# Keys and queries by one level of Strassen's recursion in a fused attention and feed-forward kernel

## The chip, the cores and the metric

The kernel runs on one core of a Trainium2 chip. The metric is the device time of one execution in microseconds (us). Engines are named as in the profile: PE is TensorE (matmuls), PEld its weight loads, DVE VectorE, ACT ScalarE, POOL GpSimd; SP issues most DMAs.

## The reference

x is 2048 x 512, with 32 heads of 16 columns and a hidden layer of 1792.

```python
x = A_x
xn = _layernorm(x, axis=-1)
s = _A_ref(xn, A_wqkv, A_wo)                  # softmax attention, 32 heads, then @ wo
g = _silu(_B_ref(xn, B_w1, B_b1, B_w2, B_b2)) # relu(xn @ w1 + b1)**2 @ w2 + b2
return x + s * g
```

Inside `_A_ref`, `qkv = x @ wqkv` (512 x 1536) gives the queries, keys and values that this change is about.

## The kernel before

All products in float32 accuracy are made from two parts: a value is split into a rounded high part and a low part (value minus high part), and a product is high x high + high x low + low x high. So one 128 x 512 output block with a contraction of 512 costs 3 x 4 = 12 matmuls of 128 x 128 on 512 columns, which accumulate in one PSUM bank (`linear`, line 112).

The front stage (lines 464 to 560) works through four chunks c of 512 tokens. For each it normalises x (`norm`, DVE, with the square root on ScalarE), transposes it on TensorE (`transpose`), and splits the result into high and low part (ScalarE casts, DVE subtracts). Then come four value tiles (`start_value`, `end_value`; stored through `vblocks`) and eight key and query blocks (`keyquery`, four groups g of 128 columns for each): 12 matmuls, a ScalarE cast to the high part, a DVE subtraction to the low part, a DMA to DRAM (`kdram`, `qdram`). PSUM has three tiles S of two banks and one bank each called lin and acc. The order of instructions is written out by hand (`manual_schedule`): every engine runs its own list in program order and waits only for data and for tiles to come free.

Between the key and query blocks lie the steps of the next chunk: `parts` is a generator over the normalisation, advanced by `next(parts)`; `split_w` makes the parts of the weights (ScalarE, GpSimd). The last chunk starts the first scores, the loads of K, Q and V (`load_ka`, `load_qa`, `load_v`), and the first pieces of the feed-forward weights (`load_piece`, `split_piece`).

The main loop follows: 64 turns of scores, exponentials (ScalarE), products with V (line 572) and, in between, the feed-forward and output matmuls (line 347), with the copies of some scores out of PSUM on DVE (line 322).

Of the kernel before, what the change touches and what calls it, by code (L numbers as in the profile page):

```python
# [48 lines left out]
def mha_ffn_kernel(ctx: ExitStack, tc: tile.TileContext, x, wqkv, wo, bx, w1, b1, w2, b2, out):  # L49
# [14 lines left out]
    xdram = [dram.tile([128, 2, 4, 512], FT, name=f"xd{c}") for c in range(3)]  # L64

# [4 lines left out]
    with tc.tile_pool(name="sb", bufs=1) as sb, tc.tile_pool(name="ps", bufs=1, space=PSUM) as ps:  # L70
        fast_path(tc, sb, ps, locals())
# [3 lines left out]
def fast_path(tc, sb, ps, env):  # L75
    nc = tc.nc
    ident, nvalid, stat = (env[n] for n in ("ident", "nvalid", "stat"))
    kdram, qdram, vdram, xdram, udram, zdram, gdram = (
        env[n] for n in ("kdram", "qdram", "vdram", "xdram", "udram", "zdram", "gdram"))
# [4 lines left out]
    BUFS = dict(S=3, KA=3, QA=2, P=8, T=2, ou=2, V=2, wr=2, u=2, st=2, mv=2, rs=2, zc=2, rc=2)  # L84
    cnt, turn, places = [0], {}, [0, 1, 2]

    def t(shape, dt, tag):

        cnt[0] += 1
        p = ps if tag in ("S", "lin", "acc") else sb  # L90
        if tag in BUFS:
            turn[tag] = turn.get(tag, -1) + 1
            n = turn[tag] % BUFS[tag]
            tag = f"{tag}{places[n] if tag == 'S' else n}"
        return p.tile(shape, dt, tag=tag, name=f"{tag}_{cnt[0]}")
# [30 lines left out]
    xload, xnorm, wraw, wsp, xT = {}, {}, {}, {}, {}  # L126

    def load_x(c):
        for i in range(2):
            a = xload[c, i] = t([128, 2, 512], FT, f"P{4 + 2 * (c % 2) + i}")  # L130
# [25 lines left out]
    def split_w(which, ks=range(4), parts="hl"):  # L156
        if which not in wsp:
            tiles = [[t([128, 2, 512], FR, f"P{8 + n}" if which == "v" and i else f"{w_tags[which]}{p}{i}")
                      for i in range(2)] for n, p in enumerate("hl")]
            wsp[which] = [[a[k // 2][:, k % 2] for k in range(4)] for a in tiles]  # L160
        for k in ks:
            raw, (h, l) = wraw[which][k // 2][:, k % 2], (p[k] for p in wsp[which])
            if "h" in parts:
                act.copy(h, raw)
            if "l" in parts:
                pool.tensor_tensor(l, raw, h.bitcast(FT), op=OP.subtract)

    def norm(c, tiles):
# [13 lines left out]
        s = t([128, 3, n], FT, "rs")  # L182
        sd, r, e = (s[:, j] for j in range(3))
# [6 lines left out]
        dve.scalar_tensor_tensor(r, e, 1.5, r, op0=OP.add, op1=OP.mult)  # L190
        for j in range(n):
            m = tiles[j]
            if m % 2 == 0:
                xnorm[c, m // 2] = t([128, 2, 512], FT, "T")
# [4 lines left out]
    def xT_tiles(c):  # L199

        if c % 2:
            xT[c] = [t([128, 4, 512], FR, f"x{p}") for p in "hl"]
        else:
            xT[c] = [t([128, 4, 512], FR, f"KA{j}") for j in range(2)]

    def transpose(c, i):
# [3 lines left out]
        pt = t([128, 4, 256], FT, "S")  # L210
        for j in range(2):
            for k in range(4):
                nc.tensor.transpose(pt[:, k, 128 * j:128 * j + 128],  # L213
                                    xnorm[c, i][:, j, 128 * k:128 * k + 128], ident)
        s = slice(256 * i, 256 * i + 256)
        if c:
            act.copy(h[:, :, s], pt)
        else:
            for j in range(2):
                act.copy(h[:, 2 * j:2 * j + 2, s], pt[:, 2 * j:2 * j + 2])  # L220
        for j in range(2):
            k = slice(2 * j, 2 * j + 2)
            dve.tensor_tensor(low[:, k, s], pt[:, k], h[:, k, s].bitcast(FT), op=OP.subtract)

    def transpose_tile(i):

        h, low = xT[0]
        pt = t([128, 4, 128], FT, "S")
# [3 lines left out]
        act.copy(h[:, :, s], pt)  # L232
        dve.tensor_tensor(low[:, :, s], pt, h[:, :, s].bitcast(FT), op=OP.subtract)

    def xpart(c, p, k):
        return xT[c][p][:, k]

    def save_xT(c):
        for p in range(2):
            sp.dma_start(xdram[c][:, p], xT[c][p].bitcast(FT))  # L240

    def start_value(c, i, tag="S", **kw):
        pv = t([128, 512], FT, tag)
# [7 lines left out]
    def end_value(c, i, v):  # L251
# [3 lines left out]
        vb = vblocks[n % 6]  # L255
        cast(act if i % 2 else dve, vb[:, :H * 17].rearrange("p (h e) -> p h e", e=17)[:, :, :DH],
# [3 lines left out]
    def keyquery(c, g, which, tag="S"):  # L260
        pk = t([128, 512], FT, tag)
        run(linear(pk, lambda p, k: wsp[which][p][k][:, 128 * g:128 * g + 128],
                   lambda p, k: xpart(c, p, k)))
        n = 2 * g + (which == "q")
        ev = t([128, 2, 512], FR, ("P2", "P3", "P4", "P5", "P6", "P7", "T", "T")[n] if c == 3 else f"P{n % 4}")
        split(ev[:, 0], ev[:, 1], pk, act, dve)
        dst = kdram[g][c // 2][:, :, 512 * (c % 2):512 * (c % 2) + 512] if which == "k" else qdram[g][c]
        sp.dma_start(dst, ev.bitcast(FT))

# [147 lines left out]
    def first(m):  # L417
# [10 lines left out]
        return [Block(lambda p, k, f=f: w[p][:, k, 128 * f:128 * f + 128], lambda p, k: x[p][:, k],  # L428
# [18 lines left out]
    def load_x_parts(c):  # L447
        xs[0] = [t([128, 4, 512], FR, f"x{p}") for p in "hl"]
        for p in range(2):
            sp.dma_start(xs[0][p].bitcast(FT), xdram[c][:, p])  # L450
# [16 lines left out]
    vblocks = [t([128, VW], FT, f"P{10 + i}") for i in range(6)]  # L467
# [4 lines left out]
    idle = t([128, 512], FT, "lin")  # L472
# [27 lines left out]
    firsts = [start_value(0, i, tag, todo=todo + late) for i, tag in enumerate(("lin", "acc"))]  # L500
    for i, n in ((0, 4), (1, 2), (0, 2), (1, 4), (0, 2), (1, 2), (0, 2), (1, 2)):
        more(firsts[i], n)
    transpose(0, 1)
    for i in range(2):
# [3 lines left out]
    for j in range(2):  # L508
        end_value(0, j, firsts[j])
    end_value(0, 2, third)  # L510
# [7 lines left out]
    parts = chain(norm(1, (0, 1)), norm(1, (2, 3)))  # L518
    for c in range(NC):
        for i in range(4):  # L520
            if c or i > 2:
                end_value(c, i, start_value(c, i))
                if c or i == 3:
                    next(parts, None)
# [546 lines left out]
```

## Time and profile before

| | |
|---|---|
| three runs | 1225.31, 1225.50, 1226.39 us; median 1225.5 |
| profiled execution, its own time | 1225.83 us |
| its span | 1224.1 us |
| granted TensorE clock | 0.998 |
| PE, DVE, ACT, POOL busy | 1213.3, 815.8, 1011.6, 278.8 us |
| last matmul of the front stage ends | 148.1 us |

The profile shows one execution, taken on the same core; the time beside the span is that of the whole launch on the device. A row of the groups has the line, engine, operation, output and input tiles, shapes and count, then busy us and mean ns of one, then the idle time before it and what ended it. A row of the timeline has start, duration, engine and line. Matmul durations overlap each other, since matmuls are pipelined; the pace is read from the chain.

### The profile page before, as it was taken

The page shows a single profiled execution, that of the slowest core. Times are in us where ns is not written, and L with a number is a line of the kernel's source. Part 1 is how long each engine was busy: PE and PEld are TensorE (multiplying, and loading weights), DVE is VectorE, ACT ScalarE, POOL GpSimd, SP SyncE. Part 2 cuts the span into 40 slices and gives each one's busy share as a digit, 9 for nine tenths or more (in the row PEclk, how much of TensorE's full clock was granted, in tenths as well). Part 3 has the DMA queues.
Part 4 walks back from the last instruction along what each step waited for, and adds up shares of the span by engine and source line. Part 5 has one row for each costly group of instructions (what it writes and reads, how often), then busy time and mean ns, then how long its engine had stood idle before and what let it go on. Part 6 is the DMA issues. An engine that isn't in the chain of part 4 may idle for free.

```text
span 1224.1 us, 24044 instructions
## 1 busy us (share of the span) xinstructions
PE 1213.3 (99%) x9925; PEld 716.3 (59%) x9925; DVE 815.8 (67%) x1302; ACT 1011.6 (83%) x1172; POOL 278.8 (23%) x222
## 2 busy tenths in 40 slices
PE   9999999999999999999999999999999999999997
PEld 8888755555555555555555555555555555555553
DVE  4542277676767775757686666676775758777776
ACT  4222489988889898888998888899898899899983
POOL 5000032122221230404022222131230403321222
PEclk9999999999999999999999999999999999999999
DMA  8675723232161223223423224151422233455434
GB/s 311 253 269 187 269 78 106 74 96 62 47 202 47 91 78 101 79 78 106 157 63 112 62 49 131 31 172 47 135 79 79 75 100 79 130 191 164 157 129 111
DMA packets 103543, 146.52 MB, mean 120 GB/s; under 512 B 42938, under 2 KB 57288, under 8 KB 101892
## 3 DMA queue, kind: packets, MB, share of 16 engines
q1 hardware_dynamic: 100772, 136.54, 35.5%
q0 software_dynamic: 2368, 7.87, 2.2%
q8 instruction: 79, 1.29, 0.4%
q10 hardware_dynamic: 288, 0.52, 0.1%
q14 instruction: 36, 0.29, 0.1%
HBM read 99.42 MB, written 45.47 MB: 118 GB/s over the span
## 4 chain that ended last, share of the span: by engine, by line
PE 99%; DVE 0%; ACT 0%; issue 0%; POOL 0%; POOLq 0%
PE acc L572 37%; PE spare L347 29%; PE S L299 15%; PE S L112 10%; PE acc L299 5%; PE lin L299 2%; PE lin L476 1%; PE S L213 1%; PE acc L112 0%; PE lin L112 0%; PE S L716 0%; DVE P L957 0%; DVE P L952 0%; PE spare L716 0%; PE S L230 0%
## 5 line engine op out<-in xcount | busy, mean ns | idle before, releaser
L303 ACT ACTIVATE P<-S 128x1024 f32<-128x1024 f32 x702 | 662.6, 1035 | 90.1 <-PE S L299 89.9
L572 PE MATMUL acc<-P,V 128*32 128x512 f32 x4096 | 453.5, 594 | 0.0
L322 DVE COPY P<-acc 128x512 f32<-128x512 f32 x322 | 222.7, 692 | 141.8 <-PE lin L299 71.3
L303 ACT ACTIVATE P<-P 128x1024 f32<-128x1024 f32 x322 | 314.5, 1082 | 0.0
L572 PEld LDWEIGHTS acc<-P,V 128*32 128x32 f32 x4096 | 126.1, 110 | 287.1 <-issue 265.5
L299 PE MATMUL S<-QA,KA 64*128 64x512 f32 x1404 | 289.7, 403 | 0.0
L322 DVE COPY P<-lin 128x512 f32<-128x512 f32 x322 | 220.5, 685 | 1.9 <-PE lin L299 0.6
L299 PEld LDWEIGHTS S<-QA,KA 64*128 64x128 f32 x1404 | 133.6, 184 | 109.8 <-issue 41.8
L105 POOL TENSOR_TENSOR wf1l<-wr,wf1h 128x1024 fp32r<-128x1024 f32 x28 | 68.4, 2443 | 289.1 <-ACT wf1h L99 112.1
L299 PE MATMUL acc<-QA,KA 64*128 64x512 f32 x322 | 127.3, 395 | 0.0
L299 PE MATMUL lin<-QA,KA 64*128 64x512 f32 x322 | 127.1, 395 | 0.0
L373 POOL MEMSET note<- 1x1 f32 x68 | 6.0, 88 | 397.7 <-PE spare L347 390.7
L347 PE MATMUL spare<-xl,wf1h 64*128 64x512 f32 x464 | 96.2, 391 | 0.0
L105 POOL TENSOR_TENSOR hl<-T,hh 128x1024 fp32r<-128x1024 f32 x28 | 80.0, 2859 | 52.9 <-DVE hh L101 51.1
L347 PE MATMUL spare<-xh,wf1l 64*128 64x512 f32 x480 | 91.6, 391 | 0.0
L347 PE MATMUL spare<-wf2l,hh 64*128 64x512 f32 x448 | 90.4, 390 | 0.0
L105 POOL TENSOR_TENSOR wf2l<-wr,wf2h 128x1024 fp32r<-128x1024 f32 x28 | 67.2, 2399 | 90.2 <-DVE wf2h L101 90.2
L598 DVE TENSOR_TENSOR ou<-acc,ou 128x512 f32<-128x512 f32 x31 | 21.4, 692 | 97.2 <-PE acc L572 85.4
L347 PE MATMUL spare<-wf2h,hl 64*128 64x512 f32 x448 | 83.5, 391 | 0.0
L347 PE MATMUL spare<-xh,wf1h 64*128 64x512 f32 x480 | 77.8, 392 | 0.0
L347 PE MATMUL spare<-wf2h,hh 64*128 64x512 f32 x448 | 72.0, 394 | 0.0
L299 PEld LDWEIGHTS acc<-QA,KA 64*128 64x128 f32 x322 | 59.3, 184 | 16.8 <-DVE P L322 2.3
(239 smaller groups left out, 1300.3 us busy)
## 6 DMA issues: line engine op xcount, KB each, us to landing
wr<-in_B_w_dram SPq DMA_DIRECT2D x56, 512.0 KB
KA<-kd SPq DMA_DIRECT2D x64, 256.0 KB
QA<-qd SPq DMA_DIRECT2D x128, 128.0 KB
kd<-P SPq DMA_DIRECT2D x15, 512.0 KB
qd<-P SPq DMA_DIRECT2D x15, 512.0 KB
u<-ud SPq DMA_DIRECT2D x15, 512.0 KB
V<-vd SPq DMA_DIRECT2D x8, 664.0 KB
vd<-P SPq DMA_DIRECT2D x16, 280.0 KB
```

The costliest lines, as they stand in the source:

```text
L105: leng.tensor_tensor(lo, src, hi.bitcast(FT), op=OP.subtract)
L112: mm(dst, lhs(a, k), rhs(b, k), start=n == 0, stop=n == len(todo) - 1)
L213: nc.tensor.transpose(pt[:, k, 128 * j:128 * j + 128], xnorm[c, i][:, j, 128 * k:128 * k + 128], ident)
L299: mm(dst, k[r, p, 128 * (kb % 8):128 * (kb % 8) + 128], q[r, p], start=True, stop=True)
L303: act.activation(ptile[i, p], src, AF.Exp, scale=SCALE)
L322: dve.tensor_copy(ptile[i, p][:, hp], sides[hp])
L347: ins = mm(bank, self.lhs(a, k)[r], self.rhs(b, k)[r], start=n == 0 and self.at[other] == 0, stop=n == len(self.todo[half]) - 1 and self.a ...
L373: f = pool.memset(note[:, notes[0]:notes[0] + 1], 0.0)
L476: mm(idle[:, :128], ident, ident, start=True, stop=True)
L572: mm(sides[0][32 * j:32 * j + 32], vq[qd][:, kb, 17 * j:17 * j + 32], ptile[i, j // 2][:, j % 2], start=first, stop=last)
L598: dve.tensor_tensor(ou, sides[0], part[0], op=OP.add)
```

## The change

- Keys and queries are made for two chunks at a time and for 256 columns at a time, as 2 x 2 blocks with a contraction of 2 x 256. Seven block products replace eight (the Winograd form of Strassen's recursion). A block product is 6 matmuls (`product`).
- For this, sums of the halves of x (T forms, `sums_x`, DVE) and of the weights (S forms, `sums_w`, DVE) are made and split into parts (ScalarE high, GpSimd low). The parts of the query S forms go to DRAM and come back for the second pair of chunks. The x forms live in `tforms`, the weight forms in `sforms`.
- The first product of the first chunk is made ahead (`first_products`, kept in SBUF by ScalarE), then `second_products` gives the first output block; `last_products` makes the other five products after the second chunk's values, adds them on DVE, and splits the results (ScalarE or, in the last group, DVE for the high part; GpSimd for the low part, which was DVE's).
- PSUM in the front stage is four banks B and four banks D; before the main loop they are closed and opened again as S0 and S1, then acc, lin and S2.
- ScalarE normalises chunks 1 to 3 and copies their values out of PSUM. The second half of the query weights is split on DVE. x is kept in four tiles rather than two, so that its DMAs are in halves. `vblocks` has three tiles rather than six.

The core of the diff:

```diff
+    BUFS = dict(S=2, D=4, B=4, KA=3, QA=2, P=8, ...)
...
-    def split_w(which, ks=range(4), parts="hl"):
+    def split_w(which, ks=range(4), parts="hl", engs=(act, pool)):
...
+        if c:
+            dve.scalar_tensor_tensor(b, mv[:, :, 0], -1.0, r, op0=OP.mult, op1=OP.mult)
...
+            if c:
+                act.activation(xnorm[c, m // 2][:, m % 2], xin[j], AF.Identity, bias=b[:, j:j + 1],
+                               scale=r[:, j:j + 1])
+                continue
...
     def transpose(c, i):
-        pt = t([128, 4, 256], FT, "S")
+        halves = [t([128, 2, 256], FT, "D") for _ in range(2)]
...
         for j in range(2):
+            act.copy(h[j][:, :, s], halves[j])
+        if c % 2:
+            plain[c, i] = halves, [t([128, 2, 2, 256], FT, f"P{2 + 2 * i + j}") for j in range(2)]
+            act.copy(plain[c, i][1][1][:, 0], halves[0])
+        for j in range(2):
+            dve.tensor_tensor(low[j][:, :, s], halves[j], h[j][:, :, s].bitcast(FT), op=OP.subtract)
...
-    def keyquery(c, g, which, tag="S"):
...
+    def product(dst, left, right):
+        todo = [(a, b, k) for a, b in ((0, 0), (0, 1), (1, 0)) for k in range(2)]
+        for n, (a, b, k) in enumerate(todo):
+            mm(dst, left[a][:, k], right[b][:, k], start=n == 0, stop=n == 5)
+
+    def sums_x(c, i, between=lambda: None):
...
+        sub(t1, f[0], h[0])
+        sub(t1, t1, l[0])
+        sub(t2, f[1], t1)
+        sub(t3, f[1], t3)
+        between()
+        def parts_of(ms):
+            for m, v in ms:
+                act.copy(tforms[m][0][:, :, s], v)
+            for m, v in ms:
+                sub(tforms[m][1][:, :, s], v, tforms[m][0][:, :, s].bitcast(FT), pool)
+        def fourth():
+            sub(t4, h[1], t2)
+            dve.tensor_tensor(t4, t4, l[1], op=OP.add)
+            parts_of([(3, t4)])
+        parts_of([(1, t2), (0, t1), (2, t3)])
+        return fourth
+
+    def sums_w(which, p, tag="gl"):
...
+        dve.tensor_tensor(s1, a21, a22, op=OP.add)
+        dve.tensor_tensor(s2, s1, a11, op=OP.subtract)
+        dve.tensor_tensor(s3, a11, a21, op=OP.subtract)
+        dve.tensor_tensor(s4, a12, s2, op=OP.subtract)
+
+    def split_sums(which, p, tags):
+        raw, parts = sraw.pop((which, p)), sum_tiles(which, p, tags)
+        split(*parts, raw, act, pool)
+        if which == "q":
+            for a, part in enumerate(parts):
+                sp.dma_start(sdram[p][:, a], part.bitcast(FT))
...
+    def first_products(c, which, ps=range(2)):
...
+            product(one, weights(which, 0, 0, p), xhalf(c, 0))
+            act.copy(t1, one)
...
+    def second_products(c, which):
...
+            product(two, weights(which, 0, 1, p), xhalf(c, 1))
...
+            dve.tensor_tensor(f, two, firsthalf[which, p], op=OP.add)
...
+    def last_products(c, which, p, temps, tags, middle, banks, parts=iter(()), end=lambda: None):
...
+            split(ev[:, 0], ev[:, 1], f, dve if middle else act, pool)
...
+        p3 = make(s[3], xhalf(c, 1))
+        add(u, make(s[1], tforms[1]), t1)
+        next(parts, None)
+        add(w, make(s[0], tforms[0]), u)
+        next(parts, None)
+        if middle:
+            middle()
+        add(t1, p3, w)
+        keep(0, (0, 1), t1)
+        p7 = make(s[2], tforms[2])
+        add(w, p7, w)
+        add(u, p7, u)
+        next(parts, None)
+        keep(1, (1, 1), w)
+        p4 = make(weights(which, 1, 1, p), tforms[3])
+        end()
+        add(u, p4, u)
+        next(parts, None)
+        keep(2, (1, 0), u)
...
+    def first_half(c):
...
+        first_products(c - 1, "k")
+        for f in second_products(c - 1, "k"):
+            f()
+        if c == 1:
+            split_sums(*kinds[0], sets[0])
+        split_sums(*kinds[1], sets[1])
...
+        if c == 1:
+            split_w("q", (2, 3), engs=(dve, dve))
+        for i in range(2):
+            first_products(c - 1, "q", (i,))
+            transpose(c, i)
...
+        fourths = [sums_x(c, 0, lambda: made.extend(second_products(c - 1, "q")))]
+        made[0]()
+        values_of_chunk(c, range(3))
+        fourths.append(sums_x(c, 1))
+        for f in fourths:
+            f()
+        values_of_chunk(c, (3,))
...
+        made[1]()
...
+    first_half(1)
+    parts = chain(norm(2, (0, 1)), norm(2, (2, 3)))
+    steps_of(parts, 2)
+    last(1, 0)
+    steps_of(parts, 1)
+    transpose(2, 0)
+    last(1, 1)
+    transpose(2, 1)
+    load_x(3)
+    parts = chain(norm(3, (0, 1)), norm(3, (2, 3)))
+    values_of_chunk(2, (0, 1))
+    more_sums(2, 2)
+    values_of_chunk(2, (2, 3))
+    more_sums(3, 3)
+    save_xT(2)
+    last(1, 2)
+    more_sums(0, 4)
+    last(1, 3)
+    steps_of(parts, 3)
+    sums_w(*kinds[1])
+    first_half(3)
...
+    def early():
+        open_banks(below, "ps2", "left", (("S0", 1024), ("S1", 1024)))
+        for q in range(2):
+            exps(0, q, scores(0, q))
...
+    for n, (which, p) in enumerate(kinds):
+        if n == 1:
+            load_qa(0, 0)
+            load_v(0)
+            load_ka(0, 1)
+        if n == 3:
+            split_piece(act)
+            open_banks(above, "ps3", "right", (("acc", 512), ("lin", 512), ("S2", 1024)))
+        last_products(3, which, p, f"P{4 + n % 2}", tags[n], *(
+            (early, ("acc", "lin", "S2", "lin", "acc"), iter(())) if n == 3 else (None, "DBBBB" if n < 2 else "BBBBB")))
```

More of the change, by code (lines that the diff above doesn't have):

```diff
@@ L509, in fast_path @@
         end_value(0, j, firsts[j])
+    next(parts[0])
+    next(parts[1])
     end_value(0, 2, third)
@@ L516, in chain, with values_of_chunk @@
             yield from g
[L518 to L524, printed above, removed]
[L525 to L530 removed]
+    def values_of_chunk(c, tiles, parts=iter(())):
+        for i in tiles:
+            end_value(c, i, start_value(c, i))
+            next(parts, None)
+            next(parts, None)
```

244 lines of the change are left out of this document (155 added, 89 removed).

## The prediction

> **What bounds the kernel now.** I read the page first: the span, the busy shares, and the chain that ended last.
>
> ```profile
> span 1224.1 us, 24044 instructions
> PE 1213.3 (99%) x9925; PEld 716.3 (59%) x9925; DVE 815.8 (67%) x1302; ACT 1011.6 (83%) x1172; POOL 278.8 (23%) x222
> ...
> PE 99%; DVE 0%; ACT 0%; issue 0%; POOL 0%; POOLq 0%
> ```
>
> TensorE is the whole chain, so time is saved only by taking matmuls away, and lost only where a matmul is made to wait. Next I read the chain in order of time for the front stage (line 112 is the matmul of values, keys and queries), and the busy time of the engines up to the last of these matmuls at 148.1 us.
>
> ```profile
> 17.32 20.86 PE S L112 x92
> 39.92 8.17 PE S L112 x36
> 48.26 19.27 PE S L112 x84
> 69.28 32.69 PE S L112 x144
> 103.71 40.81 PE S L112 x180
> ```
>
> ```profile
> 0.00:148.10 148.10, 146.56 (x685) 121.74 (x685) 61.46 (x141) 45.48 (x76) 19.16 (x34) 1.00 0.72 260
> ```
>
> The columns of the second are PE, PEld, DVE, ACT, POOL, granted clock, DMA share and GB/s. The matmuls run without a gap at 40.81 / 180 = 0.2267 us each, at full clock; the short breaks in the chain are transposes. The other engines have slack: DVE 61.5 of 148 us, ScalarE 45.5, GpSimd 19.2. That slack is what the change spends.
>
> **What it removes.** Two chunks of 512 tokens and 256 columns of keys (or queries) made 2 x 2 output blocks of 12 matmuls, 48 in all. Seven products of 6 matmuls make 42. There are 2 pairs of chunks x 2 kinds x 2 column halves = 8 such groups, so 48 matmuls go: 48 x 0.2267 = **10.9 us**, all of it on the path. Values, transposes and the matmuls of the main loop keep their number and shape.
>
> **What it adds off TensorE.** The prices:
>
> ```profile
> L105 DVE TENSOR_TENSOR P<-S,P 128x512 fp32r<-128x512 f32 x30 | 20.8, 692 | 57.6 <-ACT P L99 57.6
> L195 DVE TENSOR_SCALAR T<-P,mv,rs 128x512 f32<-128x512 f32 x16 | 8.1, 544 | 0.5
> L940 DVE TENSOR_TENSOR wf1l<-P,wf1h 128x256 fp32r<-128x256 f32 x2 | 0.8, 421 | 0.1
> L175 DVE BATCH_NORM_STATS2 st<-P 128x6 f32<-128x512 f32 x16 | 10.4, 680 | 2.7 <-DMA P<-in_A_x_dram 2.7
> L181 DVE BATCH_NORM_AGGREGATE mv<-st 128x2 f32<-128x6 f32 x16 | 2.0, 163 | 0.1
> L189 DVE SCALAR_TENSOR_TENSOR rs<-mv,rs 128x2 f32<-128x2 f32 (+1 forms) x9 | 1.4, 161 | 0.3
> L99 ACT CAST P<-S 128x512 fp32r<-128x512 f32 x30 | 17.6, 587 | 56.7 <-PE S L112 54.9 <-issue 1.7
> L164 ACT CAST hh<-wr 128x512 fp32r<-128x512 f32 x4 | 2.2, 621 | 0.0
> L99 ACT CAST wf1h<-wr 128x1024 fp32r<-128x1024 f32 x1 | 1.1, 1052 | 0.0
> L166 POOL TENSOR_TENSOR hl<-wr,hh 128x512 fp32r<-128x512 f32 x4 | 5.0, 1308 | 0.0
> L105 POOL TENSOR_TENSOR wf1l<-wr,wf1h 128x1024 fp32r<-128x1024 f32 x1 | 2.4, 2402 | 112.1 <-ACT wf1h L99 112.1
> ```
>
> - DVE loses 32 low parts (0.69 us each), 12 normalisations (0.54) and 6 value copies (0.69): 22.1 + 6.5 + 4.2 = 32.8 us. It gains 8 + 48 additions from PSUM (0.69), 24 of the x sums (0.69), 24 of the weight sums (0.42) and about 4 us of small things: 38.6 + 16.6 + 10.1 + 4 = 69.3. So 61.5 becomes about 98 us.
> - ScalarE loses 32 high parts (18.8 us) and gains 8 copies from PSUM, 8 + 21 + 16 casts from SBUF and 12 normalisations (I price these at the cast's 0.62), 6 weight casts of 1.05, 6 value copies, 4 plain copies: 4.7 + 27.9 + 7.4 + 6.3 + 3.5 + 2.3, about 52 us. So 45.5 becomes about 79 us.
> - GpSimd gains 16 + 8 + 24 low parts of 128x512 (1.31) and 6 of 128x1024 (2.40): 62.9 + 14.4 = 77 us. So 19.2 becomes about 95 us.
>
> The stage should take about 148.1 − 10.9 = 137 us, so no engine passes TensorE in the sum. What counts is who is late at single places. The sums of DVE and ScalarE were far off the path before; now the banks, the T forms (sums of x) and the S forms (sums of weights) go through three engines before a matmul can use them.
>
> **The walk.** I laid the new program order out by hand with those prices, from 21.7 us, when the first key matmul can start in both kernels.
>
> ```profile
> 17.31 0.68 DVE L101 COPY P<-lin 128x512 f32<-128x512 f32 x1
> 19.78 1.27 DVE L175 BATCH_NORM_STATS2 st<-P 128x6 f32<-128x512 f32 x2
> 21.69 1.98 PE L112 MATMUL S<-KA,wf2h 128*128 128x512 f32 x8
> 17.00:18.00 1.00, 1.00 (x6) 0.84 (x5) 0.99 (x2) 0.64 (x2) 1.00 (x2) 1.00 0.00 0
> ```
>
> Chunk 1's statistics move ahead from 19.78 to about 17.4. That costs nothing: the DMA share of 17 to 18 us is zero, so everything that was asked for had landed. The waits of matmuls that I find, without any collision of engines:
>
> 1. First query product: its bank holds the first key product, and the copy of that waits in ScalarE's queue. DVE from 17.4: two statistics 1.27, copy 0.69, aggregates 0.24, two statistics 1.27, copy 0.69, aggregates 0.24, the scale in small steps 1.05: 22.9. ScalarE then: two normalisations 1.24, value copy 0.59, two query casts 1.2: 25.9; two more normalisations, 27.2; the copy, 27.8. TensorE comes at 21.7 + 24 x 0.2267 = 27.2. **0.6 us**.
> 2. Third value tile of chunk 1: its bank holds a query product. ScalarE from 27.8: a copy, two high parts, two weight casts, 32.0; then for each half of the transposed chunk a copy, two high parts and a plain copy, 2.35: 36.7. DVE's low parts end at 37.0, four subtractions 2.8, then the addition that frees the bank: 40.4. TensorE: the transposes end at 32.7, two query products 2.7, two value tiles 5.4: it wants the bank at 40.9. Nothing, 0.5 us to spare.
> 3. The T forms. ScalarE's casts stand behind the copy of that third tile (ready 43.6, copied 44.4): 45.0, 45.6, 46.2; GpSimd's low parts of 1.3 end at 46.3, 47.6, 48.9, and those of the fourth form at 50.2 and 51.5. TensorE ends the values at 46.3, makes one product without a T form, and wants these at 47.7, 49.0, 50.4 and 51.8. Nothing, with 1.4 us to spare and 0.3 at the last. Chunk 3 repeats places 2 and 3 with some more room.
> 4. Third value tile of chunk 2, behind low parts that stand behind the additions of a last group of products, by the same reckoning: **0.4 us**.
> 5. First half done again for chunk 2: pair one ends at 86.6 on TensorE, two key products end at 89.3, and the third wants the bank of the seventh product of the group before. DVE, coming from weight sums at 85.6: addition 0.69, aggregates 0.24, addition 0.69, scale 1.05, three additions 2.1: 90.4. **1.1 us**.
> 6. Third group of the last pair: five products in four banks, the fifth wanted after 4 x 1.36 = 5.4 us, its bank freed by DVE after 5.7: **0.4 us**.
>
> Together 2.5 us. Sixteen transposes, made in two lots, are priced at the 1.75 us of their break in the chain (48.26 + 19.27 = 67.53 to 69.28). Everything else I cost at nothing: the parts of S are made some 10 us ahead, the loads of x, the first K, Q and V of the loop have 10 us or more, and the extra 4 MB of S forms to DRAM and back go out in stretches with DMA to spare (mean share 0.72 above). The stage's end:
>
> ```profile
> 148.06 0.50 PE L299 MATMUL S<-QA,KA 64*128 64x512 f32 x2
> 149.59 0.50 PE L299 MATMUL acc<-QA,KA 64*128 64x512 f32 x1
> 148.84 0.69 DVE L105 TENSOR_TENSOR T<-acc,T 128x512 fp32r<-128x512 f32 x1 [2.97 <-ACT T L99]
> ```
>
> The loop wants bank acc 1.53 us after its first matmul. By my order the last addition frees it 1.3 us after that: no wait, but only 0.2 to spare.
>
> **The unknown: DVE and GpSimd against each other.** In the front stage of before GpSimd is mostly idle, so the loop has to tell.
>
> ```profile
> 390.73 2.39 POOL L105 TENSOR_TENSOR wf1l<-wr,wf1h 128x1024 fp32r<-128x1024 f32 x1 [5.71 <-issue]
> 391.94 2.26 DVE L424 TENSOR_TENSOR T<-T 128x1024 f32<-128x1024 f32 x1
> 395.01 3.96 POOL L105 TENSOR_TENSOR hl<-T,hh 128x1024 fp32r<-128x1024 f32 x1 [1.89 <-DVE hh L101]
> 395.56 1.15 DVE L638 SCALAR_TENSOR_TENSOR y<-T,y 128x1024 f32<-128x1024 f32 x1
> ```
>
> The square at 391.94 ends at 394.20, 1.08 us after GpSimd's instruction ended (393.12): it stood still until then. In the second pair GpSimd, released at 395.01, needs 3.96 for 2.4 us of work and ends 2.26 after DVE's instruction with two SBUF inputs (396.71). So the two exclude each other, and a DVE train once running is not broken by a waiting GpSimd. The Trainium skill says it as a rule ("SBUF — State Buffer", section "Who interferes with whom"): a DVE instruction with two SBUF inputs and a GpSimd instruction that reads SBUF share a port, and the second to come blocks until the first is done; the rows agree, and the rule speaks against this change.
>
> The change brings such trains: weight sums (6 trains of 4), x sums (4 single ones, 4 pairs) and the split of half the query weights (one train of 4), against a GpSimd that is busy 95 / 137 = 0.7 of the time. If each train waits one whole GpSimd instruction, and GpSimd then each train, my walk becomes: place 2 costs 1.0; place 3 costs 2.3 (first form late by 1.2, the last by another 1.1); place 2 and 3 again in the last pair 3.3; a weight form ahead of the first query group 0.5; place 5 another 1.3. That is 8.4 us more. A train meets GpSimd busy 0.7 of the time and on average halfway through, so I take a third: 2.8 us. Stalls together 2.5 + 2.8 = 5.3; bounds 2.5 and 10.9.
>
> **The sum.** 10.9 − 5.3 = 5.6 us less. The profiled execution took 1225.83 us by the clock beside its span of 1224.1 (1.7 outside); 1225.83 − 5.6 = 1220.2. The median of the three runs, 1225.5, lies 0.3 below that execution: **1219.9 us**.
>
> **The rivals.**
> - *Nothing collides.* The trains fall into GpSimd's pauses. Stalls 2.5, time 1225.5 − 8.4 = 1217.1. For it: the late fourth forms and the additions between the subtractions leave 1.4 us of margin at place 3. Against it: GpSimd's 0.7. Chance 0.3.
> - *Everything collides once.* Stalls 2.5 + 8.4 = 10.9: about 1225.5, no change. Against it: it needs the worst meeting each time. Chance 0.13.
> - *Slower: the split of the query weights.* If DVE and GpSimd take turns instruction by instruction, the four DVE instructions on weights 2 and 3 (from about 29.7 us) alternate with two key low parts of 1.31 and two weight sums of 2.40 and end near 39.6; the query products want them at 32.7. That is 7 us, and together with the collisions above (some 9 of whose 10.9 us remain) 16 us of stalls against 10.9: 1230.6. It decides once the stalls pass 10.9 + 2.5 us. Against it: the row of 3.96 us, where DVE did not take turns. For it: only one such meeting is in the trace. Chance 0.17.
> - The forecast itself, 1218 to 1223: 0.4.
>
> About 0.2% (2.5 us) is what a measurement of this kernel can tell from no change. Faster by more: the forecast and the clean case, 0.70; within: 0.13; slower: 0.17. The range reaches from all 10.9 us gained with nothing lost (1214.6) to just above no change, 1227.
>
> **What would show it right or wrong.** Right: 48 fewer matmuls of 512 columns, pace still 0.2267, loop's first matmul near 142.5 instead of 148.06, its turns unchanged; TensorE idle in the front in a few gaps of 0.3 to 1.5 us that end on GpSimd (T forms) or DVE (banks); GpSimd near 95 us there. DVE instructions with two SBUF inputs stretched to 1 us and more next to GpSimd show the collisions. Wrong: a gap of several us before the second query products near 33 us ending on DVE (the slower rival); a gap at the loop's start; or the loop itself longer, which I take as untouched.

## The result

| | before | after |
|---|---|---|
| median | 1225.5 us (5 runs, 1225.17 to 1226.39) | 1231.36 us (5 runs, 1230.90 to 1232.14) |
| profiled execution, its own time; its span | 1225.83; 1224.1 us | 1232.14; 1230.4 us |
| loop's first matmul starts | 148.06 us | 152.74 us |

The change makes the kernel slower: the ratio of the times is 1.0048 with a 95% interval of 1.0033 to 1.0063. The forecast was 1219.9 us, with a range up to 1227.0, so the sign is wrong and the time lies outside the range.

The same parts of the page after the change (span, busy share of each engine, and the engines' shares of the chain that ended last):

```profile
span 1230.4 us, 24207 instructions
PE 1209.7 (98%) x9877; PEld 712.9 (58%) x9877; DVE 874.4 (71%) x1369; ACT 1041.4 (85%) x1225; POOL 356.3 (29%) x268
PE 87%; DVE 1%; issue 1%; DMA 0%; POOL 0%; SPq 0%; ACT 0%; DVEq 0%; POOLq 0%
```

The 48 matmuls are gone (9925 to 9877), but TensorE is no longer the whole chain. Next the stage up to the loop's start (columns as before: PE, PEld, DVE, ACT, POOL, clock, DMA share, GB/s), one stretch of the last products from the chain of waits, and the loop's start from the timeline:

```profile
0.00:152.70 152.70, 141.91 (x635) 113.25 (x635) 118.74 (x207) 75.17 (x130) 93.75 (x78) 0.99 0.73 261
132.06 9.79 PE B L291 x42
152.74 0.50 PE L471 MATMUL S<-QA,KA 64*128 64x512 f32 x2
```

The stage ends 4.7 us later instead of 10.9 us earlier: 15.6 us were lost in it, and the remaining span grew by another 1.6 (1224.1 − 148.06 = 1076.0; 1230.4 − 152.74 = 1077.7). DVE is busy 118.7 us there where I had reckoned 98; ScalarE (75 for 79) and GpSimd (94 for 95) came as reckoned. And the matmul's pace is 9.79 / 42 = 0.2331 us, not 0.2267. Who made TensorE wait, in us (total, times, longest; two waits of 1.4 and 0.3 us at the kernel's start and end are left out, since the kernel before has them too):

```profile
PE B L291 <- DVE xl L415: 4.1, 2, 2.7
PE D L234 <- ACT T L204: 1.7, 1, 1.7
PE B L291 <- DVE hl L172: 1.6, 1, 1.6
PE D L291 <- POOL P L110: 0.8, 1, 0.8
PE B L117 <- ACT y L320: 0.6, 1, 0.6
PE B L291 <- POOL P L311: 0.3, 1, 0.3
PE B L291 <- DVE hh L106: 0.2, 1, 0.2
```

Together 9.3 us. Where DVE's 20 extra us went is seen in its groups, kept apart by shape (busy us, mean ns of one):

```profile
L311 DVE TENSOR_TENSOR P<-D,P 128x512 f32<-128x512 f32 x8 | 5.2, 686 | 0.1
L326 DVE TENSOR_TENSOR P<-P,KA 128x512 f32<-128x512 f32 x4 | 5.7, 1426 | 0.1
L172 DVE TENSOR_TENSOR hl<-wr,hh 128x512 fp32r<-128x512 f32 x2 | 4.4, 2206 | 0.1
L106 DVE CAST hh<-wr 128x512 fp32r<-128x512 f32 x2 | 1.9, 956 | 0.0
L194 DVE SCALAR_TENSOR_TENSOR rs<-rs 128x2 f32<-128x2 f32 x6 | 4.6, 771 | 0.2
L195 DVE SCALAR_TENSOR_TENSOR rs<-mv,rs 128x2 f32<-128x2 f32 x6 | 4.2, 696 | 0.2
```

The first row, with one input in PSUM (tile D), keeps the 0.69 us of the prediction. The other rows, whose inputs are all in SBUF, are stretched: 1426 and 2206 ns for the same 512 columns, and 771 and 696 ns for steps on 128x2 numbers that took 161 ns before. The timeline shows how in the set of steps that was hit hardest, DVE first and then GpSimd (start, duration):

```profile
51.88 0.47 DVE L194 SCALAR_TENSOR_TENSOR rs<-rs 128x2 f32<-128x2 f32 x1
52.38 1.21 DVE L195 SCALAR_TENSOR_TENSOR rs<-mv,rs 128x2 f32<-128x2 f32 x1
53.63 1.21 DVE L196 SCALAR_TENSOR_TENSOR rs<-rs 128x2 f32<-128x2 f32 x1
54.87 1.19 DVE L198 SCALAR_TENSOR_TENSOR rs<-mv,rs 128x2 f32<-128x2 f32 x1
51.04 2.53 POOL L311 TENSOR_TENSOR V<-P,V 128x512 fp32r<-128x512 f32 x2
53.54 2.51 POOL L397 TENSOR_TENSOR P<-P 128x512 fp32r<-128x512 f32 x2
```

Each 0.16-us step starts while a GpSimd instruction of 1.3 us runs and lasts until its end, four times in a row. Not every step meets this: of the 24 such steps of chunks 1 to 3, 9 are stretched (for up to 2.07 us) and 15 keep 0.16 us. ScalarE's normalisation needs the last of them, and the transposes need that: they start 1.7 us late. After that gap the matmuls are slow (timeline of TensorE, then the windows, whose third number from the right is the granted clock):

```profile
56.97 1.36 PE L234 MATMUL D<-ident,T 128*128 128x128 f32 x8 [1.74 <-ACT T L204]
60.39 2.27 PE L291 MATMUL B<-u,P 128*128 128x512 f32 x6
58.00:59.00 1.00, 1.00 (x7) 0.86 (x5) 0.90 (x2) 0.46 (x1) 0.00 (x0) 0.77 0.22 86
60.00:61.00 1.00, 1.00 (x4) 0.80 (x3) 0.93 (x4) 0.81 (x2) 0.60 (x2) 0.50 0.00 0
62.00:63.00 1.00, 1.00 (x6) 0.79 (x6) 0.53 (x3) 0.37 (x1) 0.19 (x1) 1.00 0.98 383
```

The clock falls to half for 3 to 4 us. The 12 matmuls from 58.09 to 62.50 took 4.41 us instead of 12 x 0.2333 = 2.80, so the gap cost another 1.6 us, and 1.9 with the eight transposes ahead of them.

### The profile page after: what moved, and what is told of

Same layout as the page of the kernel before. It is cut to its first block, busy times and chain, and to the rows that moved or that the text cites. A ratio compares the mean times of both kernels' runs of the same rounds, so it can differ in the third digit from the quotient of the medians.

```text
span 1230.4 us, 24207 instructions
## 1 busy us (share of the span) xinstructions
PE 1209.7 (98%) x9877; PEld 712.9 (58%) x9877; DVE 874.4 (71%) x1369; ACT 1041.4 (85%) x1225; POOL 356.3 (29%) x268
## 4 chain that ended last, share of the span: by engine, by line
PE 87%; DVE 1%; issue 1%; DMA 0%; POOL 0%; SPq 0%; ACT 0%; DVEq 0%; POOLq 0%
PE acc L811 36%; PE S L519 28%; PE S L471 14%; PE acc L471 4%; PE lin L471 2%; PE B L291 1%; DMA hl<-gd 0%; PE S L954 0%; PE B L117 0%; PE lin L291 0%; SPq L841 0%; PE acc L291 0%; POOL P L311 0%; POOL T L311 0%; POOL u L311 0%
## 5 line engine op out<-in xcount | busy, mean ns | idle before, releaser
L519 PE MATMUL S<-xl,wf1h 64*128 64x512 f32 x464 | 96.5, 391 | 0.0
L519 PE MATMUL S<-xh,wf1l 64*128 64x512 f32 x480 | 92.0, 391 | 0.0
L519 PE MATMUL S<-wf2l,hh 64*128 64x512 f32 x448 | 90.9, 390 | 0.0
L519 PE MATMUL S<-wf2h,hl 64*128 64x512 f32 x448 | 83.8, 391 | 0.0
L519 PE MATMUL S<-xh,wf1h 64*128 64x512 f32 x480 | 78.0, 392 | 0.0
L519 PE MATMUL S<-wf2h,hh 64*128 64x512 f32 x448 | 72.1, 394 | 0.0
```

Of the source, the lines that this page charges most:

```text
L519: ins = mm(bank, self.lhs(a, k)[r], self.rhs(b, k)[r], start=n == 0 and self.at[other] == 0, stop=n == len(self.todo[half]) - 1 and self.a ...
```

## The experiments

Theory A: DVE instructions that read SBUF twice (or copy from SBUF to SBUF) and GpSimd instructions exclude each other one by one, and TensorE waits for what gets late by it. Against it stood: the forms or the work itself are too much (a longer queue without stretching), too little DMA, and the half clock as main cause.

**1. GpSimd reads nothing (x1_noport).** Its front-stage subtractions become pairs of memsets; the low parts are left out.

```diff
-                sub(tforms[m][1][:, :, s], v, tforms[m][0][:, :, s].bitcast(FT), pool)
+                blank(tforms[m][1][:, :, s])      # two memsets on GpSimd
...
-        split(*parts, raw, act, pool)
+        cast(act, parts[0], raw)
+        blank(parts[1])
```

> The changed kernel with every GpSimd subtraction of the front stage (weights, T forms, S forms, keys and queries; the low parts) put in place by two memsets of the same tile, about 2 x 0.55 = 1.1 us for 1.3 us, which read nothing from SBUF. It leaves out the low parts, so part of the products adds zero. Theory A (collisions: DVE instructions with two SBUF inputs stand still while GpSimd reads SBUF; in the changed kernel's trace these DVE instructions are some 25 us longer than undisturbed): the small scale steps go back to 0.16 us, the gaps of TensorE ahead of the second query product (1.7 us), ahead of the transposes of chunk 2 (1.9 us and the half clock behind it, 1.6 us) and ahead of the first key products of chunk 2 (1.6 and 2.8 us) go, and the time falls by 8 to 12 us to about 1219 to 1223. Theory B (DVE simply has too much to do in the first 60 us): the gaps stay within a half, time above 1227.

1217.13 us, ratio 0.993 (0.9914 to 0.9947) to the kernel before. GpSimd is still busy 75.8 us up to the loop, yet DVE is back at 94.0, its small steps and sums at their old length (by shape, mean ns last; only the two casts of the query split stay long, 612 ns), and the waits of TensorE hold only the two at the start and the end that the kernel before has as well:

```profile
L204 DVE SCALAR_TENSOR_TENSOR rs<-rs 128x2 f32<-128x2 f32 x6 | 1.0, 161 | 0.2
L336 DVE TENSOR_TENSOR P<-P,KA 128x512 f32<-128x512 f32 x4 | 2.8, 693 | 0.1
PE B L661 <- POOL ident masks.py:199: 1.4, 1, 1.4
PE S L966 <- ACT wf1h L1186: 0.3, 1, 0.3
```

All the waiting goes with the collisions, as Theory A has it: 14.2 us lie between this kernel and the changed one, more than the 8 to 12 expected. In the profiled executions 1.0 us of it is the start: the first key product begins at 20.94 us here and at 21.94 in the changed kernel, ahead of any collision. The run also takes 18 us off GpSimd and spares it the wait for ScalarE's casts, so the 1.1 us of waiting that ended on GpSimd may have gone by that alone; the other 8.2 ended on DVE and ScalarE. The hand-made order was sound; without collisions it beats the kernel before.

**2. The small steps alone (x2_small).** The scale is made by `tensor_scalar` with the second number as a pointer, on one column at a time, so that only one operand is a stream: eight instructions instead of four.

```diff
-        dve.scalar_tensor_tensor(e, r, -0.5, r, op0=OP.mult, op1=OP.mult)
...
+        for j in col:
+            ts(e[:, j], r[:, j], -0.5, r[:, j], op0=OP.mult, op1=OP.mult)
...
```

> The changed kernel with the four small steps of the normalisation's scale (128x2, two SBUF inputs) written as eight of 128x1 with one tensor input and a scalar read by pointer; the same arithmetic. Theory A, with the small steps as the main place: they took 0.34 to 0.77 us each instead of 0.16, 9 us of DVE in all, 3.5 us of it just ahead of the transposes of chunk 2; with one tensor input they take 0.16 us, that gap (1.9) and the half clock behind it (1.6) go, the gaps ahead of the keys of chunk 2 shrink by about 2: time about 1226 (1224 to 1228). If it is the sums' trains that cost: no change within 1 us.

1223.86 us, ratio 0.9985 (0.9975 to 0.9995). The steps, by shape:

```profile
L197 DVE TENSOR_SCALAR rs<-rs 128x1 f32<-128x1 f32 x12 | 2.0, 208 | 0.2
PE B L297 <- DVE xl L421: 0.8, 1, 0.8
PE B L297 <- DVE hl L172: 1.6, 1, 1.6
```

Twice as many instructions, 208 ns each beside the same GpSimd, no longer wait. The wait for xl falls from 4.1 to 0.8 us, the one before the transposes is gone with its half clock. 7.5 of the 11.5 us that my forecast missed went with these four lines, a little more than expected.

**3. The half clock alone (x3_fill).** Eight matmuls of the identity that nothing reads are put ahead of the late transposes.

```diff
+    idle = t([128, 512], FT, "D")
+    keep_clock(8)
     transpose(2, 0)
```

> The changed kernel with eight small matmuls of the identity (128 columns) ahead of the transposes of chunk 2, in a bank of their own, where TensorE waits 1.9 us and then runs 3.5 us at half the clock. If the idle time is what halves the clock: the granted clock stays 1.00 through 58 to 62 us and the time falls by 1.6 us less whatever the small matmuls take past the gap, to about 1229.8 to 1230.5. If the clock falls for another reason: it still falls, and the time is the changed kernel's or up to 1 us more.

1229.64 us, ratio 1.003 (1.0018 to 1.0043), 1.7 us below the changed kernel. The window after the gap:

```profile
57.00:63.00 6.00, 5.78 (x28) 4.39 (x27) 5.02 (x12) 2.40 (x5) 2.59 (x2) 1.00 0.38 147
```

The clock stays whole there. But it falls elsewhere: behind the gap of 2.7 us ahead of the key products, at full clock in the changed kernel, it is now at half (one window of this kernel, then the same of the changed one):

```profile
102.00:103.00 1.00, 1.00 (x4) 0.75 (x3) 1.00 (x2) 0.04 (x1) 1.00 (x2) 0.50 0.97 406
102.00:103.00 1.00, 1.00 (x6) 0.80 (x5) 0.96 (x2) 1.00 (x3) 1.00 (x2) 1.00 0.00 0
```

So in the profiled executions the filled gap gives 1.5 us and the other stretch takes about 1.4 back. From the first key product to the loop only 0.7 us are gained (130.12 for 130.80); that the median fell by 1.7 us, about the 1.6 reckoned above, is luck, and does not show that the filling is worth this much. The half clock is a follow-up cost of a gap, met once in the changed kernel's trace, and not the main cost.

**4. The floor, and the forms unused (x4_floor, x6_unused).** In the first no sums, forms or splits of them are made and the last products use plain parts; in the second all are made and none is used. Keys and queries are other numbers in both.

```diff
 x6_unused, in last_products:
-        add(u, make(s[1], tforms[1]), t1)
...
+        s = [weights(which, m // 2, m % 2, p) for m in range(4)]
+        forms = [xhalf(c, 1)] * 4
+        add(u, make(s[1], forms[1]), t1)
```

> The changed kernel with all sums of x and of weights left out, with their splits, copies and their way through DRAM; the five last products take plain parts of x and weights instead, so keys and queries are other numbers. All matmuls, the additions on DVE and the splits of results stay. If the seven products are worth 48 x 0.2267 = 10.9 us when nothing makes TensorE wait: about 1215 to 1217. If the additions from PSUM and the new banks cost by themselves: above 1220.

> The changed kernel with all sums made, split and stored as they are, but the five last products take plain parts of x and weights, so keys and queries are other numbers. Nothing of TensorE waits for a T or S form; banks, values, transposes and the query split still come through DVE and ScalarE. If what hurts is lateness of the forms themselves: about 1217 (as x4_floor, 1215.9). Theory A says the forms cost 0.8 + 0.3 us only and the rest comes from the queue of DVE: 1228 to 1230. The pace of the last products: 0.2333 us per matmul in the changed kernel and in x1_noport, 0.2267 in x4_floor. If the load of the other engines slows it, it stays 0.233 here; if it is the operands, 0.2267.

1215.92 us (ratio 0.9919, 0.9902 to 0.9935) and 1229.24 us (1.0029, 1.0018 to 1.004). The floor confirms the 10.9 us: 9.8 of them show. The second keeps the waits (xl 4.4 us, T 1.6, hl 1.6) though no matmul waits for a form any more. So the T and S forms' own lateness was worth at most the 2.1 us between this kernel and the changed one; what came late in the main was DVE's queue, and behind it the banks and the normalised x. The chain also shows the pace (x4_floor, then x6_unused), which is not a matter of using the forms:

```profile
117.15 9.54 PE B L290 x42
130.21 9.81 PE B L291 x42
```

0.2271 us a matmul in the floor, 0.2336 with the same operands and the sums made beside them.

**5. GpSimd's load in the kernel before (b1_poolload).** Three dead subtractions behind each key and query block of the first two chunks (and two memsets of their inputs), no other change.

```diff
+                for _ in range(3 if c < 2 else 0):
+                    pool.tensor_tensor(junk[2], junk[0], junk[1], op=OP.subtract)
```

> The kernel before, with 48 GpSimd subtractions of 128x512 added that nothing uses (three behind each key and query block of the first two chunks), so GpSimd is busy in the front stage as it is in the changed kernel, and nothing else differs. Theory A (VectorE's steps that read two SBUF operands take turns with a GpSimd instruction, whatever their own length): the 128x2 scale steps, 161 ns in the kernel before, show a mean of 0.5 to 1.2 us; TensorE hardly waits, since VectorE has room there, and the time is within 1.5 us of the kernel before. Rival A2 (the short steps were late in the changed kernel for another reason, such as its own longer queue): they keep 160 to 200 ns. On the pace: if the busy GpSimd is what slows TensorE's matmuls from 0.2267 to 0.2333 us, the matmuls of this kernel's front stage show 0.230 or more; if not, they stay at 0.227.

1232.48 us, ratio 1.0052 (1.0036 to 1.0068): as slow as the changed kernel, with work added on GpSimd alone. By shape, and from the timeline and the chain:

```profile
L188 DVE SCALAR_TENSOR_TENSOR rs<-rs 128x2 f32<-128x2 f32 x6 | 4.5, 746 | 0.2
L189 DVE SCALAR_TENSOR_TENSOR rs<-mv,rs 128x2 f32<-128x2 f32 x6 | 1.0, 161 | 0.2
L195 DVE TENSOR_SCALAR T<-P,mv,rs 128x512 f32<-128x512 f32 x12 | 16.0, 1370 | 0.4
42.41 0.66 PE L213 MATMUL S<-ident,T 128*128 128x128 f32 x4 [3.01 <-DVE T L195]
54.63 19.27 PE S L112 x84
```

The stretch was as expected for the first and the third step of a set (746 and 973 ns in the mean); the second (line 189) keeps its 161 ns in every set. It starts right behind the first, some 0.03 us ahead of GpSimd's next instruction (29.74 against 29.77, 39.44 against 39.47), and the third then waits for that instruction's end. So the one that starts first goes undisturbed. That TensorE would hardly wait was wrong: the normalisation too, 544 ns before, takes 1370, and the transposes wait 3.8 us for it, with a half clock after that (8 matmuls in 3.28 us for 1.81). The pace is the old one while GpSimd is fully busy: 84 matmuls from 54.63 us take 19.27 us, as in the kernel before (from 48.26). GpSimd's load does not slow the matmuls.

**6. Other places for the sums (x5_ports, x7_ports_dma).** On top of x2_small, the key weight sums go to GpSimd, the whole query split goes early to ScalarE and GpSimd, and the split of the second key sums goes behind the transposes; x7_ports_dma also moves three DRAM stores later.

```diff
-    sums_w(*kinds[0])
+    sums_w(*kinds[0], eng=pool)
...
-            split_w("q", (2, 3), engs=(dve, dve))
...
+    split_w("q", (2, 3))
```

> The changed kernel with the collisions taken out where they hurt, results as in the reference: the small scale steps with one tensor input (as in x2_small), the sums of the key weights on GpSimd rather than DVE (both times), all query weights split early on ScalarE and GpSimd rather than the second half on DVE, and the split of the second key sums behind the transposes. x2_small still made TensorE wait 2.1 us for the query split on DVE, 0.8 for a bank behind the key sums on DVE, 0.8 for a query form, 0.4 and 0.3 in the last pair. Theory A: the first two go; time 3 to 4 us below x2_small, 1219.5 to 1221. Theory B (DVE's load): the work left on DVE falls only by some 7 us of sums, the waits come back elsewhere, time within 1.5 us of x2_small's 1223.9. If GpSimd's longer queue now is what is late: above 1224.

> x5_ports with three stores to DRAM moved back by some 10 us each: the query forms (behind the values of chunk 2, and behind the third last group) and x of chunk 2 (behind the fourth). In x2_small a value copy on ScalarE waits 6.9 us for an earlier value's store, which stands behind them in the DMA queue (DMA share 0.95 to 1.04 from 75 to 85 us), and the second query form is 0.8 us late behind that copy. If so: that wait falls below 2 us, the gap of 0.8 goes, and the time is 0.8 to 1 us below x5_ports. If the form is late through GpSimd: no change.

1224.57 (ratio 0.9991, 0.9982 to 1.0) and 1225.49 us (0.9999, 0.999 to 1.0008): both missed what was hoped for (1219.5 to 1221, and 0.8 to 1 us below x5_ports). The time of x5_ports fits two of its other cases, DVE's load and a longer GpSimd queue that is late; the trace below shows the second. In x7_ports_dma the 0.8 us that end on GpSimd's query form stay, as its rival "late through GpSimd" has it. The gap at the query split went, and a new one came. Timeline of x5_ports, ScalarE, DVE and TensorE:

```profile
90.21 1.05 ACT L104 CAST KA<-gl 128x1024 fp32r<-128x1024 f32 x1 [5.04 <-POOL gl L349]
91.49 0.17 DVE L193 RECIPROCAL rs<-rs 128x2 f32<-128x2 f32 x1 [3.99 <-ACT rs L191]
94.82 1.56 PE L297 MATMUL B<-KA,wf2h 128*128 128x512 f32 x4 [2.53 <-DVE xl L421]
```

ScalarE's cast waits for GpSimd's sums, the square root of the normalisation is queued behind the cast, DVE waits for the root, and the additions that free the bank are queued behind DVE's reciprocal. The wait was handed on by three queues.

**7. These two waits mended (x8_tuned).** On top of x5_ports that cast moves behind the transposes of the next step, and both query sums run ahead of the value tiles that follow, the second in a raw tile of its own.

```diff
+        if c == 3:
+            split_sums(*kinds[0], sets[4])
...
-    more_sums(0, 4)
+    sums_w(*kinds[0], eng=pool)
```

> The kernel with the scale steps in the form with a pointer and the sums spread over GpSimd, with two waits of it mended: both query sums of the second form run right behind each other on VectorE ahead of the value tiles that follow, in a raw tile of their own, and the ScalarE cast of the first key sums of the third pair moves behind the transposes, so that the square root no longer waits behind GpSimd's sums. Theory A (TensorE waits where VectorE or GpSimd is late with a tile, and each such wait costs its own length and a half-clocked stretch behind it): the gaps of 2.5 and 0.8 us go, waits of TensorE between 5 and 150 us sum to under 1.5 us, the time is 1219 to 1221 us. Rival B (the time lost is not in the waits but in a slower pace of TensorE under the denser stage): the gaps go and the time stays within 1223.5 to 1225.5 us, with matmuls of 0.233 us in the last products. Rival C (each mended place hands the wait on to the next step of the same queue): a new gap of over 1 us shows elsewhere before 150 us, and the time stays at 1223 to 1225 us.

1220.47 us, ratio 0.9955 (0.9941 to 0.997). TensorE's largest waits inside the stage are now

```profile
PE B L297 <- POOL P L317: 0.4, 1, 0.4
PE D L240 <- ACT T L210: 0.3, 1, 0.3
PE B L297 <- POOL V L317: 0.3, 1, 0.3
```

so the time moved with the waits, as Theory A has it. This is the change with a gain, 0.45%.

**8. The pace (p1_nosums, p2_noforms, x9_aligned).** Both start from x6_unused: one without the weight sums, one without the activation forms.

```diff
 p1_nosums, in sums_w:
-        dve.tensor_tensor(s1, a21, a22, op=OP.add)
...
+        pass
 p2_noforms, in sums_x:
-        sub(t1, f[0], h[0])
...
+        plain.pop((c, i), None)
+        between()
+        return lambda: None
```

> The kernel with all forms made and unused (last products on plain parts, 0.2333 us a matmul) without the sums of the weights, their splits and their DRAM stores and loads; queries and keys are other numbers. Asked: which work goes with the pace of 0.2333 us a matmul of the last products, where the kernel without any sums or forms has 0.2271 us. If the weight sums (VectorE's adds beside the matmuls, the tiles they fill, their transfers) set it, the last products go at 0.227 us here; if the activation forms do, at 0.233; if it is neither alone, something between or 0.233 in both this and its partner. In every case VectorE's queue is shorter by about 28 instructions, and the waits of TensorE for xl in 94 to 102 us (4.4 us with all work) shrink.

> The same without the activation forms (VectorE's subtractions, ScalarE's casts and GpSimd's subtractions of the four forms of each second half), the weight sums made and unused; queries and keys are other numbers. If the activation forms set the pace, the last products go at 0.227 us here; if the weight sums do, at 0.233. TensorE's wait for the transposes near 57 us and for hl near 35 us, which come from the scale steps and the query split taking turns with GpSimd, stay where GpSimd still works beside them (hl, 1.6 us) and go where its forms are gone (57 us).

1220.17 us (ratio 0.9958, 0.9939 to 0.9978) and 1227.02 us (1.0002, 0.9991 to 1.0013). The last products on the same plain parts in both, from the chain:

```profile
120.94 9.53 PE B L291 x42
125.72 9.81 PE B L291 x42
```

p1_nosums is at the old pace, 9.53 / 42 = 0.2269 us, with GpSimd fully busy (5.00 of the 5 us from 115 us on); p2_noforms is at the slow one, 0.2336, even in a stretch in which DVE and GpSimd do nothing (118 to 120 us). So it isn't their load. What differs is where the tiles lie: with the weight sums a tile of 5312 bytes a partition (V0) comes ahead of xh, xl, u and y, and these start at 32 bytes past a multiple of 128; without, they start at 96 past, as xh and xl do in the kernel before. The last run puts 64 unused bytes behind V0 and V1 in x8_tuned.

> The kernel with the tuned order, and 64 bytes of unused space in each SBUF partition behind each of the two tiles V0 and V1, nothing else changed. Without them every tile allocated behind V0 (whose 5312 bytes are no multiple of 128) starts at 32 bytes past a multiple of 128: the activation tiles xh and xl and the forms u and y, which TensorE streams, among them; in the kernel before these tiles start at 96 past a multiple. In the two kernels that leave out one kind of forms, the placement was the only difference that went with the pace: 0.2267 us a matmul with 96, 0.2333 with 32, while the work beside it did not. Theory P (the start of the streamed tile sets the pace): the products of keys and queries of the second form go at 0.227 to 0.229 us a matmul instead of 0.2333, about 240 x 0.0066 = 1.6 us, and the time is 1218 to 1219.2 us. Rival Q (the pace comes from something else that the sums of the weights bring): the products stay at 0.233 us and the time at 1220 to 1221 us.

1219.70 us, ratio 0.9945 (0.9931 to 0.9959), the fastest that computes all: 0.8 us below x8_tuned. Two groups of its timeline, with weights in tiles that start at 64 past and at 96 past:

```profile
121.18 1.56 PE L303 MATMUL B<-u,P 128*128 128x512 f32 x6
122.58 1.56 PE L303 MATMUL B<-y,P 128*128 128x512 f32 x6
128.13 1.52 PE L303 MATMUL B<-u,P 128*128 128x512 f32 x6
129.49 1.52 PE L303 MATMUL B<-y,P 128*128 128x512 f32 x6
```

Starts 1.40 us apart are 0.2333 us a matmul, 1.36 apart 0.2267, with the same u and y. The time lies between the two that were expected (up to 1219.2, and from 1220). So the expectation fell in part: placing the streamed tile was not enough, since most weight sums still lay at 64 past. In the long groups of these front stages 0.2267 shows where both operands start at 96 past a multiple of 128, and 0.229 to 0.233 where one starts at 96 and the other at 32 or 64. The few matmuls with both at 32 (a last group, 0.224 to 0.236 between starts) don't tell whether 96 itself or the equal start counts; nine with both at 64 in the kernel before, 0.228 to 0.233 apart, speak rather against the equal start. Why is open, and a kernel with all sums placed so was not run. Unexpectedly the gain lay in the loop, which starts at 141.9 us in both kernels: the rest of the span behind the loop's first matmul is 1076.1 us as in the kernel before, 1077.1 in x8_tuned. Which tile did that is open too.

## Why the prediction was wrong, point by point

- *What it removes.* Right: 48 matmuls; the floor kernel shows 9.8 us. That the clean one came to 1217.13 against the 1217.1 of the rival "nothing collides" is partly luck: its waits came out at zero instead of 2.5 us, which paid for the slower pace.
- *Prices and sums.* Right for GpSimd (though 19.2 + 77 is 96, not 95; measured 93.8) and ScalarE. The step that failed is in DVE's: the small steps were priced at 1.05 us a set from rows measured while GpSimd was idle, and were left out of the list of trains that collide; in the changed kernel a set takes up to 4.2 us (51.88 to 56.06), and the form that avoids this takes 7.5 of the 11.5 us away. The list also left out the casts. The Trainium skill ("SBUF — State Buffer", section "Who interferes with whom"), which I had drawn on, also names casts and `tensor_scalar` in a two-port mode as colliders; the cast at 956 ns (413 for casts of this shape elsewhere in the kernel before) and the normalisation at 1370 for 544 agree.
- *"A DVE train once running is not broken by a waiting GpSimd."* Wrong. I read it from one meeting in the loop, where a single GpSimd instruction met a single DVE one, which says nothing of trains. By their start times GpSimd's instruction even came first there (395.01 against 395.56) and still gave way; that pair stays unexplained, and only the first pair agrees with the rule. The rows of 51.88 to 56.06 show that a train is broken: a step that starts while a GpSimd instruction runs lasts until its end, however short the step. With this reading the meeting is priced per instruction, not per train: four short steps can cost four GpSimd instructions, as in this set, or none, as in another.
- *The waits.* Of six places, none came at its price. Place 5 was foreseen (1.1 us for late additions in the second pair), but behind stretched steps it became two gaps of 1.4 and 2.7; place 1 became 1.8 us at the query split. The gap before the transposes, 1.7 us, was in no list. Place 6 comes to 0.3 by its own numbers, not 0.4. Forecast stalls 5.3, measured 9.3.
- *"TensorE at full clock."* The walk charged a gap its own length. Half clock after one of them: 1.9 us with the transposes.
- *Pace 0.2267, and the loop untouched.* Wrong by an estimated 240 x 0.0066 = 1.6 us in the products (the two kernels without inner waits, x1_noport and x4_floor, lie 1.25 us apart between the first key product and the loop, 117.34 and 116.09) and by 1.6 us in the loop, of which 1.0 went with the placement of tiles in x9_aligned.
- Of the 10.2 us by which the loop starts later than forecast (152.74 for 142.5), 4.0 are more waiting. A gap also costs about 0.26 us more than its row says: the start at 95.38 us, behind 1.43 us of waiting, comes 1.59 later against the same matmul of x1_noport, and the next one another 0.11. Over the eight gaps that is 2.2 us. The half clock is 1.9. Another 1.8 are in x1_noport too: from the first key product to the loop it takes 117.3 us where the walk without waits has 142.5 − 5.3 − 21.7 = 115.5, mostly pace. Together 9.9; the start, 0.2 us later than 21.7, makes 10.1 of it.
- *The slower rival.* Its mechanism, DVE and GpSimd held up instruction by instruction, was the right one. Its time, 1230.6, was near by luck: it put 7 us at the query split, where 1.8 were measured, and the rest came from places and costs that it did not have. With 0.17 it was underrated, because one row was taken as evidence against it.

## What to carry to other kernels

Before work is moved to an idle GpSimd, list every DVE instruction of the stretch that reads only SBUF, the tiny ones first, and charge each with up to one whole GpSimd instruction (9 of 24 small steps paid here). Ways out that worked here are the form with a pointer on single columns (208 ns) and an input in PSUM (0.69 us for 512 columns); on 512 columns from SBUF to SBUF the form with pointers was stretched too, 1370 for 544 ns. Then look for what is queued behind the instruction that gets late, on each engine in turn, before moving it: x5_ports moved the wait instead of removing it. A stage in which TensorE never waited has margins that no busy share shows: 62.5 us of dead GpSimd work cost the kernel before 6.7 us.

## What the runs showed of the hardware that I had not expected

- A DVE step of 0.16 us that starts while a GpSimd subtraction runs lasts until that ends (up to 2.07 us); one that starts 0.03 us ahead of the next subtraction keeps 161 ns. The form with a pointer on one column takes 208 ns beside the same GpSimd.
- Whether a gap halves the clock differs between executions of nearly the same code. The gap of 1.7 us ahead of the transposes did so for 3 to 4 us in the changed kernel, and one of 1.6 us at the same place in x6_unused did not. The gap of 2.7 us ahead of the key products did not in the changed kernel, but did in x3_fill (and 2.6 us in x6_unused). The Trainium skill ("TensorE: Matmul & The Clock Gate", "What's actually happening") speaks of a window of about 3.4 us that runs freely; these traces agree in length and in the chance of it, and that a gap shorter than the window can be enough is shown here.
- The start of a tile in SBUF went with a change of the matmul's pace by 2.9%, also while DVE and GpSimd did nothing.
